# Memory sums from 32-column products, with a new instruction order, in a fused attention and FFN kernel on one Trainium2 core

## The chip, the cores and the metric

The kernel runs on one NeuronCore of a Trainium2 chip. Five engines work side by side and wait for each other through semaphores: TensorE (PE, matrix products into the accumulators of PSUM), VectorE (DVE), ScalarE (ACT), GpSimd (POOL) and SyncE (SP, which only issues DMA transfers here). The metric is device time in microseconds, the median of several executions.

## The reference, cut to what matters

Two pairs of layers follow each other with residual additions: memory attention (A), gated FFN (B), A, B, with the same weights both times. 2048 rows of 512 are worked in four segments of 512 rows; 32 heads of 16 columns.

```python
q, k, v = heads of (layernorm(x) @ wq, wk, wv)
phi = lambda t: jnp.where(t > 0, t + 1.0, jnp.exp(t))
for s in range(N):                    # N = 4 segments
    p = softmax(qs @ ks.T * scale + mask)
    a_dot = p @ vs
    pq = phi(qs)
    num = einsum('bhld,bhde->bhle', pq, M)
    den = einsum('bhld,bhd->bhl', pq, z)[..., None] + 1e-06
    o = g * num / den + (1.0 - g) * a_dot
    pk = phi(ks)
    M = M + einsum('bhld,bhle->bhde', pk, vs)     # the memory sum
    z = z + einsum('bhld->bhd', pk)
x = x + o @ wo
x = x + (gelu(layernorm(x) @ w_gate) * (layernorm(x) @ w_up)) @ w_down
```

M is one 16x16 matrix per head. The change concerns how M is summed, and the order of all the work.

## The kernel before, in words

The whole program is emitted by one function, `order`. It walks through the work with a planner written out by hand: a model clock for each engine (`Clocks`, `Engine`), a list of PE work items (`Item`) with due times and conditions of readiness, and lists of jobs for DVE, ACT, POOL and SP with a slack each. At each step it takes a ready item with the earliest due time and emits its instructions. So the order on every engine, and which engine takes a job that two could do (an eviction from PSUM, a mask, masked copies of k), comes out of the numbers in `POLICY`. On the chip the order is fixed; only semaphores decide the times.

A step `k` (0 to 7) is one segment of one layer pair. Its items on PE are: the q, k and v products; score rounds in row tiling (L938, four products of 16 or 32 rows beside each other); the P·V items, called `flush` (L954), in four column tiles of 32; the memory items `den` (phi(q) by z) and `num` (phi(q) by M); `upd`, the memory sum; `wo`; then `gate`, `up` and `down` of the FFN. `product` (L471 and L476) emits a 128-row product either whole (L476) or as four products in column tiles (L471), after the tiling that PE is in. Where nothing is ready, the planner puts a filling product on a tile of ones, `warm`, into the stream.

The memory sum (`upd_item`, from L853) runs for segments 0 to 2 of each layer. phi(k) is made on ACT and DVE, turned by DMA into `phik` (rows on partitions), and 16 products of 128x128x128 give four blocks of 128x128 in one PSUM bank: each block holds the products of eight heads with eight heads, of which only the eight 16x16 diagonal pieces are wanted. DVE adds the four blocks to `macc` (128x512, float32), and multiplies by the block mask `bd` into `mblk` (L878), which `num` reads; `zcols` (L882) does the same for z, from `zacc`. In segment 0 the mask is applied straight from PSUM, and `macc` is copied afterwards (L893); later segments add to `macc` first (L895).

Layernorm (`Norm`): statistics on DVE (L514, L522), the scale on POOL (L527, L532), `xn` on DVE or POOL (L544), and then a turn into `xnT`, by PE transposes (L586, with evictions at L461 and L462) or by a DMA transpose from SP's queue (L437). `by_pe` decides: the FFN norms of steps 0, 1 and 7, and the input norms up to step `pe_turns`.

SP's queue, in order: the loads of x and of the attention weights, the copies of v into `vz` (L701), the loads of wo, w_gate, w_up and w_down, and the DMA transposes of `phik`, `xnT` and `amT` between them.

## Time and profile before

| | |
|---|---|
| median of 3 runs | 544.17 us (544.15 to 544.77) |
| span of the profiled execution, first to last instruction | 542.6 us (the page gives no other time of that execution) |
| granted TensorE clock | 1.000 of full speed |
| HBM read, written | 9.70 MB, 2.10 MB |
| the costliest group on ACT | exponentials of the scores, 288 of 1026 ns |
| the costliest group on POOL | masks of 256 and 512 columns, 192 together, 579 ns each |
| the costliest groups on PE | 512-column products, 379 ns each by the records, which overlap |

A row of a group reads: line, engine, operation, output <- inputs, partitions x elements, count | busy us, mean ns of one | idle time of the engine just before them, and what ended it. A row of the timeline reads: start and length in us, engine, line, operation, count of merged instructions. Products on PE overlap in the records, so what a run of them takes is read from its start to the start of the next run. Some product records are missing (9271 of 9332).

### The profile page before, as it was taken

The page shows a single profiled execution, that of the slowest core. Times are in us where ns is not written, and L with a number is a line of the kernel's source. Part 1 is how long each engine was busy: PE and PEld are TensorE (multiplying, and loading weights), DVE is VectorE, ACT ScalarE, POOL GpSimd, SP SyncE. Part 2 cuts the span into 40 slices and gives each one's busy share as a digit, 9 for nine tenths or more (in the row PEclk, how much of TensorE's full clock was granted, in tenths as well). Part 3 has the DMA queues.
Part 4 walks back from the last instruction along what each step waited for, and adds up shares of the span by engine and source line. Part 5 has one row for each costly group of instructions (what it writes and reads, how often), then busy time and mean ns, then how long its engine had stood idle before and what let it go on. Part 6 is the DMA issues. An engine that isn't in the chain of part 4 may idle for free.

```text
span 542.6 us, 21272 instructions
## 1 busy us (share of the span) xinstructions
PE 527.1 (97%) x9271; PEld 274.9 (51%) x9332; DVE 443.1 (82%) x816; ACT 434.4 (80%) x540; POOL 305.9 (56%) x359
## 2 busy tenths in 40 slices
PE   8999989999999999999999999999999999999997
PEld 4454455454545444544544555545465456555444
DVE  7898999799988999879987998889586797786342
ACT  6999989988998989989799798996879977930320
POOL 4897786369846788349993468716753265300000
PEclk9999999999999999999999999999999999999999
DMA  8306510610331123310312250211420105100001
GB/s 268 98 13 192 117 23 17 171 35 20 51 50 24 24 40 61 41 38 9 41 32 50 33 71 4 40 33 23 79 52 3 22 13 89 24 3 25 16 0 40
DMA packets 64784, 26.94 MB, mean 50 GB/s; under 512 B 49074, under 2 KB 64690, under 8 KB 64690
## 3 DMA queue, kind: packets, MB, share of 16 engines
q1 hardware_dynamic: 64400, 25.31, 22.7%
q8 instruction: 73, 1.20, 0.9%
q10 hardware_dynamic: 290, 0.26, 0.2%
q14 instruction: 21, 0.17, 0.1%
HBM read 9.70 MB, written 2.10 MB: 22 GB/s over the span
## 4 chain that ended last, share of the span: by engine, by line
PE 83%; DVE 12%; issue 2%; DMA 2%; ACT 0%; POOL 0%; SPq 0%; DVEq 0%; ACTq 0%
PE ps L476 44%; PE ps L471 25%; PE ps L938 7%; PE ps L954 6%; DVE st L514 2%; DVE x_sb L1027 1%; DVE xn L544 1%; DVE byq L971 1%; DMA phik<-e 1%; DVE phiq L745 1%; DVE mv L522 1%; DMA x_sb<-in_A_x_dram 0%; DMA amT<-am 0%; DVE e L745 0%; ACT pt L1398 0%
## 5 line engine op out<-in xcount | busy, mean ns | idle before, releaser
L1398 ACT ACTIVATE pt<-ps 128x1024 bf16<-128x1024 f32 x288 | 279.1, 1026 | 44.3 <-PE ps L938 40.3
L1345 POOL TENSOR_SCALAR_AFFINE_SELECT pt<-pt 128x256 bf16<-128x256 bf16 (+1 forms) x192 | 108.6, 579 | 117.1 <-ACT pt L1398 110.4
L1092 DVE TENSOR_TENSOR gel_sb<-gel_sb,ps 128x512 bf16<-128x512 bf16 x112 | 75.2, 681 | 34.0 <-PE ps L476 25.0
L476 PE MATMUL ps<-xnT,wu_sb 128*128 128x512 bf16 x287 | 66.8, 379 | 1.4 <-issue 1.1
L476 PE MATMUL ps<-xnT,wg_sb 128*128 128x512 bf16 x261 | 62.6, 379 | 1.3 <-issue 0.5
L764 POOL TENSOR_SCALAR e<-e 128x512 bf16<-128x512 bf16 x37 | 57.6, 1557 | 1.6 <-ACT e L741 0.6
L971 DVE STREAM_TRANSPOSE byq<-ps 128x512 f32<-128x512 f32 x64 | 45.0, 706 | 16.3 <-PE ps L954 15.6
L476 PE MATMUL ps<-wd_sb,gel_sb 128*128 128x512 bf16 (+1 forms) x293 | 56.8, 340 | 1.3 <-issue 1.0
L1027 DVE TENSOR_TENSOR x_sb<-x_sb,ps 128x512 bf16<-128x512 bf16 (+1 forms) x68 | 42.8, 640 | 16.5 <-PE ps L476 14.8
L1350 POOL TENSOR_SCALAR_AFFINE_SELECT pt<-pt 64x1024 bf16<-64x1024 bf16 x40 | 47.7, 1194 | 15.1 <-ACT pt L1398 13.8
L471 PE MATMUL ps<-wd_sb,gel_sb 128*32 128x512 bf16 (+1 forms) x792 | 47.1, 378 | 0.6 <-issue 0.6
L476 PEld LDWEIGHTS <-wu_sb 128*128 128x128 bf16 x301 | 28.3, 98 | 33.8 <-issue 0.7
L471 PE MATMUL ps<-xnT,wg_sb 128*32 128x512 bf16 x700 | 42.4, 380 | 0.1
L514 DVE BATCH_NORM_STATS2 st<-x_sb 128x6 f32<-128x512 bf16 x60 | 40.4, 673 | 0.1
L476 PEld LDWEIGHTS <-wg_sb 128*128 128x128 bf16 x273 | 25.3, 98 | 29.1 <-DVE byq L971 0.6
L476 PEld LDWEIGHTS <-gel_sb 128*128 128x128 bf16 x306 | 28.3, 98 | 22.6 <-issue 1.1
L954 PE MATMUL ps<-pt,vaug 128*32 128x256 bf16 (+2 forms) x1344 | 34.8, 238 | 0.3 <-POOL pt L1345 0.3
L471 PE MATMUL ps<-xnT,wu_sb 128*32 128x512 bf16 x588 | 34.1, 379 | 0.0
L417 POOL TENSOR_SCALAR kx<-kf,masks 128x512 bf16<-128x512 bf16 x20 | 33.0, 1649 | 1.2
L1151 ACT ACTIVATE gel_sb<-gel_sb 128x2048 bf16<-128x2048 bf16 (+1 forms) x21 | 33.2, 1643 | 0.0
L954 PEld LDWEIGHTS <-vaug 128*32 128x32 bf16 x1344 | 27.9, 97 | 10.5 <-issue 2.3
L544 DVE TENSOR_SCALAR xn<-x_sb,mv,rs 128x512 bf16<-128x512 bf16 x58 | 31.4, 592 | 2.2 <-POOL rs L532 1.9
(149 smaller groups left out, 877.0 us busy)
## 6 DMA issues: line engine op xcount, KB each, us to landing
vz<-vaug SPq DMA_DIRECT2D x14, 136.0 KB, 2.7
wg_sb<-in_B_w_gate_dram SPq DMA_DIRECT2D x8, 224.0 KB, 4.0
wu_sb<-in_B_w_up_dram SPq DMA_DIRECT2D x8, 224.0 KB, 5.0
wd_sb<-in_B_w_down_dram SPq DMA_DIRECT2D x7, 256.0 KB, 4.7
x_sb<-in_A_x_dram SPq DMA_DIRECT2D x3, 512.0 KB, 6.6
out_dram<-x_sb SPq DMA_DIRECT2D x12, 128.0 KB, 1.9
xnT<-xn SPq DMA_TRANSPOSE x40, 2.5
wk_sb<-in_A_wk_dram SPq DMA_DIRECT2D x2, 256.0 KB, 5.1
```

The lines of the kernel that those rows point to most:

```text
L471: nc.tensor.matmul(out[r], lhsT=lhsT[:, r], rhs=rhs, start=start, stop=stop, tile_position=(0, 32 * c))
L476: nc.tensor.matmul(out, lhsT=lhsT, rhs=rhs, start=start, stop=stop)
L514: nc.vector.bn_stats(out=self.st6[:, 0, :], in_=x_sb[:, self.tt0 + j, :])
L764: lambda eng: eng.tensor_scalar(out=e[0][:], in0=e[0][:], scalar1=1.0, scalar2=None, op0=ALU.min), summed)
L938: nc.tensor.matmul(ps_all[:, bank, o + c0:o + c0 + n], lhsT=lhsT, rhs=self.q[rows, b, q0:q0 + n], start=True, stop=True, tile_position=(32 ...
L954: nc.tensor.matmul(ps()[32 * j:32 * j + 32, q0:q0 + n], lhsT=va[:, ki * VW + g:ki * VW + g + 32], rhs=pt_all[:, places[i], j, c0:c0 + n], ...
L971: nc.vector.transpose(out=self.byq[:, par, :, :].rearrange("p a c -> p (a c)"), in_=ps()[:])
L1027: ck.dve.post(ck.made(), slack, (0.15 + 0.00104 * (c1 - c0), lambda: nc.vector.tensor_tensor(out=xt, in0=xt, in1=ps()[:, 0:c1 - c0], op=AL ...
L1092: ck.dve.post(ck.made(), NORMAL, (0.683, lambda: nc.vector.tensor_tensor(out=g, in0=g, in1=ps()[:], op=ALU.mult), lambda t: (ps.read(t), e ...
L1345: nc.gpsimd.affine_select(out=view, in_=view, pattern=[[0, 4], [0, n], [1, C]], compare_op=ALU.is_ge, fill=0.0, base=C, channel_multiplier=-1)
L1350: nc.gpsimd.affine_select(out=view, in_=view, pattern=[[0, 4 * TPS], [1, C]], compare_op=ALU.is_ge, fill=0.0, base=0, channel_multiplier=-1)
L1398: nc.scalar.activation(out=pt_all[:, s0:s0 + 2, 2 * p:2 * p + 2, :].rearrange("p r h c -> p h r c"), in_=ps_all[:, pair[0]:pair[1] + 1, :] ...
```

## The change

The 16 products of a memory sum become 64: for each block of 128 rows and each group of eight heads, four products of 32 columns, one in each column tile, each multiplying 32 columns of phi(k) (two heads) with the 32 columns of v of the same two heads. The result is 128x128 for all 32 heads (`pairs`), so that `macc` shrinks to 128x128. `spread` then makes the 128x512 `mblk` with the block mask, reading `macc` four times over; segment 0 does so too.

```diff
-    macc = cst.tile([P, 4, P], F32, name="macc")
+    macc = cst.tile([P, 4, 32], F32, name="macc")
...
-            def m(c):
-                j, b = divmod(c, 4)
-                product(blocks()[:, b, :], self.phik[:, j, b * P:(b + 1) * P],
-                        by_head(self.vaug)[:, j, 4 * b:4 * b + 4, :, 0:DH], c == 0, c == n_mm - 1)
+            def m(j, b):
+                ck.tiling("columns")
+                for c in range(4):
+                    nc.tensor.matmul(pairs()[32 * c:32 * c + 32, b, :], lhsT=self.phik[:, j, b * P + 32 * c:b * P + 32 * c + 32],
+                                     rhs=by_head(self.vaug)[:, j, 4 * b + c, :, 0:DH], start=(j == b == 0),
+                                     stop=(j == TPS - 1 and b == 3), tile_position=(0, 32 * c))
+                ck.count += 4
...
-                def gated(src):
-                    return lambda: nc.vector.tensor_tensor(out=made[0][:], in0=src(),
-                                                           in1=bd[:].unsqueeze(1).to_broadcast([P, 4, P]), op=ALU.mult)
+                def spread():
+                    nc.vector.tensor_tensor(out=made[0][:].rearrange("p b (c d) -> p b c d", d=32),
+                                            in0=macc[:].unsqueeze(2).to_broadcast([P, 4, 4, 32]),
+                                            in1=bd[:].rearrange("p (c d) -> p c d", d=32).unsqueeze(1).to_broadcast([P, 4, 4, 32]),
+                                            op=ALU.mult)
...
                 if self.s == 0:
-                    steps = [(0.154, lambda: nc.vector.tensor_copy(out=zacc[:], in_=self.zk[:]), kept),
-                             (0.683, gated(blocks), None),
-                             (Port(0.2), z, told),
-                             (0.683, lambda: nc.vector.tensor_copy(out=macc[:], in_=blocks()), psm.read)]
+                    first = [(0.283, lambda: nc.vector.tensor_copy(out=macc[:], in_=pairs()), psm.read),
+                             (0.154, lambda: nc.vector.tensor_copy(out=zacc[:], in_=self.zk[:]), kept)]
...
+                ck.dve.chain(ck.made(), pol.mem_slack, *first, (Port(0.69), spread, None), (Port(0.2), z, told))
...
-            items.append(Item(lambda: k + pol.upd_due, ready, [(Clocks.MM[128], lambda c=c: m(c)) for c in range(n_mm)],
+            items.append(Item(lambda: k + pol.upd_due, ready,
+                              [(Clocks.SMALL, lambda j=j, b=b: m(j, b)) for j in range(TPS) for b in range(4)],
```

Beside it nearly all numbers of `POLICY` are new, so that the order on each engine is made anew. Some of them are counts: `pe_turns` from 2 to 0 (the input norms of steps 1 and 2 are turned by DMA), `gelu_tiles` from 4 to 7 (tiles of the FFN in one gelu instruction), `hold` from 8 to 3 (score rounds wait until this many gelu tiles are left), `cap` from 4 to 2.

Counted in the instructions of both kernels: products 9332 before, 10075 after; changes of the tiling 301 and 300; column-tiled steps of 512 columns 662 and 808; PE transposes 96 and 64 (16 of each in the first norm); filling products of 128 columns, a column-tiled four counted once, 31 and 44; DMA transposes on SP's queue 88 and 96. In the stretch from the first residual add of the first `wo` to the last `xnT` copy, DVE has the spread, `zcols` and `macc` before, and a second P·V eviction with its reciprocal and scaling after; the spread and `zcols` come behind it.

More of the change, by code (lines that the diff above doesn't have):

```diff
@@ L69 @@
 POLICY = dict(
-    flush_wait=31.348, piece_slack=5.108, kb_slack=25.115, mem_slack=-15.103, margin=2.314, qk_due=0.572,
-    e_q=-1.218, e_k=1.714, exp_slack=-25.107, e_slack=9.023, phi_slack=17.383, gelu_slack=6.274,
-    act_evict=8.464, first_evict=0.965, gate_step=0.061, up_due=-0.553, up_step=0.062, down_due=2.078,
-    down_step=0.526, upd_due=0.786, kb_act=6.552, vz_slack=-10.454, x_dve=-0.565, v0_due=-1.4, x1_at=-45.234,
-    x2_at=18.289, x3_at=24.819, x3_load=-3.83, direct=4, gelu_tiles=4, look=1.769, lag=0.5, wv_at=8.591,
-    xn_pool=7.037, kb_pool=5.303, cut_pool=1.107, at_pool=10.661, pe_turns=2, gate_due=0.765, shun=0.534,
-    col_gap=3.33, hold=8, early=4.123, starve=0.308, near=-1.576, cap=4, soon=9.685, columns=0)
+    flush_wait=60.178, piece_slack=2.474, kb_slack=40.846, mem_slack=-55.59, margin=2.052, qk_due=-2.997, e_q=-1.628,
+    e_k=2.444, exp_slack=-52.211, e_slack=213.844, phi_slack=26.757, gelu_slack=17.711, act_evict=-7.207,
+    first_evict=15.014, gate_step=70.271, up_due=-0.803, up_step=0.121, down_due=2.855, down_step=15.464,
+    upd_due=-0.036, kb_act=30.625, vz_slack=-37.946, x_dve=-2.928, v0_due=-11.201, x1_at=-44.439, x2_at=17.127,
+    x3_at=25.097, x3_load=11.502, direct=4, gelu_tiles=7, look=4.219, lag=0.576, wv_at=-5.253, xn_pool=39.635,
+    kb_pool=0.131, cut_pool=-3.745, at_pool=5.073, pe_turns=0, gate_due=2.262, shun=0.829, col_gap=3.113, hold=3,
+    early=122.612, starve=0.322, near=-0.26, cap=2, soon=21.81, columns=0)
 CHANGES = {
@@ L854, in upd_item, with pairs @@
             psm = Psum()
-            def blocks():
-                return psm().rearrange("p (b d) -> p b d", d=P)
-            n_mm = 4 * TPS
+            def pairs():
+                return psm()[:, 0:4 * 32].rearrange("p (b d) -> p b d", d=32)
             def ready():
@@ L889, in done @@
                 if self.s == 0:
-                    steps = [(0.154, lambda: nc.vector.tensor_copy(out=zacc[:], in_=self.zk[:]), kept),
-                             (0.683, gated(blocks), None),
-                             (Port(0.2), z, told),
-                             (0.683, lambda: nc.vector.tensor_copy(out=macc[:], in_=blocks()), psm.read)]
+                    first = [(0.283, lambda: nc.vector.tensor_copy(out=macc[:], in_=pairs()), psm.read),
+                             (0.154, lambda: nc.vector.tensor_copy(out=zacc[:], in_=self.zk[:]), kept)]
                 else:
-                    steps = [(0.683, lambda: nc.vector.tensor_tensor(out=macc[:], in0=macc[:], in1=blocks(),
+                    first = [(0.283, lambda: nc.vector.tensor_tensor(out=macc[:], in0=macc[:], in1=pairs(),
                                                                      op=ALU.add), psm.read),
                              (0.154, lambda: nc.vector.tensor_tensor(out=zacc[:], in0=zacc[:], in1=self.zk[:],
-                                                                     op=ALU.add), kept),
-                             (Port(0.69), gated(lambda: macc[:]), None),
-                             (Port(0.2), z, told)]
-                ck.dve.chain(ck.made(), pol.mem_slack, *steps)
-            items.append(Item(lambda: k + pol.upd_due, ready, [(Clocks.MM[128], lambda c=c: m(c)) for c in range(n_mm)],
+                                                                     op=ALU.add), kept)]
+                ck.dve.chain(ck.made(), pol.mem_slack, *first, (Port(0.69), spread, None), (Port(0.2), z, told))
+            items.append(Item(lambda: k + pol.upd_due, ready,
+                              [(Clocks.SMALL, lambda j=j, b=b: m(j, b)) for j in range(TPS) for b in range(4)],
                               done, kind="upd", ps=psm, after=("phik", k, 3)))
```

## The prediction

> **What bounds the kernel now.** I read the head of the page first, then the chain of waits, then the windows.

> ```profile
> span 542.6 us, 21272 instructions
> PE 527.1 (97%) x9271; PEld 274.9 (51%) x9332; DVE 443.1 (82%) x816; ACT 434.4 (80%) x540; POOL 305.9 (56%) x359
> ...
> PE 83%; DVE 12%; issue 2%; DMA 2%; ACT 0%; POOL 0%; SPq 0%; DVEq 0%; ACTq 0%
> ```

> TensorE (PE) is busy 97% of the span and carries 83% of the chain that ended last. So a change is worth what it takes out of PE's own row of work, or out of the waits of PE that are left. The windows show where those are.

> ```profile
> 60.00:84.00 24.00, 21.71 (x505) 12.82 (x509) 23.33 (x47) 21.40 (x28) 19.32 (x21) 1.00 0.19 31
> ...
> 130.00:140.00 10.00, 8.51 (x211) 5.13 (x212) 9.77 (x21) 8.36 (x11) 7.50 (x11) 1.00 0.01 3
> 140.00:300.00 160.00, 157.52 (x2894) 80.06 (x2915) 139.46 (x250) 146.74 (x178) 107.80 (x116) 1.00 0.24 39
> 300.00:460.00 160.00, 157.53 (x3082) 83.21 (x3095) 131.00 (x230) 135.13 (x162) 88.94 (x110) 1.00 0.23 39
> ```

> Columns after the stage: PE, weight loads, DVE, ACT, POOL. Between 140 and 460 us PE idles 5 us in 320, a floor of 1.5% spread evenly. Two stretches idle far more: 2.3 us of 24 before the first FFN and 1.5 us of 10 before the second. In both DVE is busy 97 to 98%: there PE waits for layernorm on DVE. Everywhere else the sum is PE's own instructions.

> **Part 1: the products of the memory sums.** Six sums (segments 0 to 2 of both layers) are made. Now each is 16 products of 128 columns; afterwards each is 64 products of 32 columns, four column tiles at a time. The cost of a run is read from its start to the start of the next row in the timeline.

> ```profile
> 264.42 1.14 PE L476 MATMUL ps<-vaug,phik 128*128 128x128 bf16 x16
> 265.40 1.46 PE L476 MATMUL ps<-wd_sb,gel_sb 128*128 128x512 bf16 x5
> ...
> 395.11 1.19 PE L471 MATMUL ps<-vaug,phik 128*32 128x128 bf16 x64
> 396.07 0.65 PE L471 MATMUL ps<-wd_sb,gel_sb 128*32 128x512 bf16 x7
> ...
> 288.41 0.69 PE L471 MATMUL ps<-zcols,phiq 128*32 128x8 bf16 x64
> 288.93 1.27 PE L471 MATMUL ps<-xnT,wu_sb 128*32 128x512 bf16 x20
> ...
> 145.04 0.56 PE L476 MATMUL ps<-zcols,phiq 128*128 128x8 bf16 x16
> 145.46 2.10 PE L476 MATMUL ps<-xnT,wg_sb 128*128 128x512 bf16 x8
> ```

> A sum costs 0.98 us whole and 0.96 us in column tiles now. No product 32 columns wide in four column tiles is in the trace. Nearest below is the 8-wide one: 64 in 0.52 us, 8.1 ns each. Nearest above is the 128-wide one, 0.96 us, which would be no gain. I take 0.52 us, since 32 columns are much nearer to 8 and the narrow run is plainly held by issue and not by its columns: 6 x (0.96 - 0.52) = **-2.6 us**, bounds -2.6 and 0; a loss would need column tiles that don't overlap (rival b).

> [...]

> **Part 2: what the sum becomes on DVE.** The accumulation shrinks from 512 to 128 columns, the masked spread always starts from SBUF.

> ```profile
> L878 DVE TENSOR_TENSOR mblk<-macc,bd 128x512 bf16<-128x512 f32 x4 | 3.9, 970 | 0.0
> ...
> L789 DVE SCALAR_TENSOR_TENSOR rdm<-ps,tmp_e 128x128 f32<-128x128 f32 x6 | 1.7, 281 | 0.0
> ...
> L878 DVE TENSOR_TENSOR mblk<-ps,bd 128x512 bf16<-128x512 f32 x2 | 1.3, 667 | 0.0
> L893 DVE COPY macc<-ps 128x512 f32<-128x512 f32 x2 | 1.3, 666 | 0.0
> ```

> A 128-column read of PSUM takes 0.28 us (row L789) in place of 0.67, six times: -2.3 us of DVE; two spreads go from 0.67 to 0.97: +0.6. The spread stands one instruction later in segment 0, so its readers (the phi of the next segment) see it some 0.3 us later. All of this lies beside dense products: 0 on PE, except in the stretch before the first FFN (part 5). With that cover gone, the 1.7 us that DVE saves would come off the end too, and the later spread would put 0.3 us back per layer.

> **Part 3: products that change form or vanish.** The new order has 300 changes between whole, row and column tiling where the old has 301: 0. It makes 146 more of the 512-column steps in column tiles; the chain of waits prices both forms.

> ```profile
> 473.44 22.45 PE ps L471 x416
> ...
> 515.74 10.96 PE ps L476 x50
> ```

> 416 / 4 = 104 column steps in 22.45 us are 0.216 us each; 50 whole ones in 10.96 us are 0.219, with some records missing: 0.

> The input norms of segments 1 and 2 are no longer turned on PE but by DMA (80 transposes of this line become 48).

> ```profile
> 20.52 1.06 PE L586 MATMUL ps<-ident,xn 128*128 128x128 bf16 x16
> 21.41 0.28 PE L476 MATMUL ps<-warm 128*128 128x128 bf16 x2
> ```

> 16 took 0.89 us; 32 fewer: **-1.8 us**, and eight evictions less on ACT and DVE, beside PE's work: 0.

> The filling products (on a tile of ones, issued where the plan has nothing else) grow from 31 to 44 (column ones counted in fours).

> ```profile
> L476 PE MATMUL ps<-warm 128*128 128x128 bf16 x19 | 2.6, 220 | 0.0
> ```

> A 128-column product costs 0.06 us as above: 13 x 0.06 = **+0.8 us**; the waits that they stand in are counted below. At most, 2.6 / 19 = 0.14 each, +1.8.

> **Part 4: the start of segment 1, now behind eight DMA transposes on SP's queue.** SP's new order is one transpose, the two vz copies, six transposes, then the wo load.

> ```profile
> 17.72 1.40 DVE L544 TENSOR_SCALAR xn<-x_sb,mv,rs 128x512 bf16<-128x512 bf16 x3
> ...
> 18.84 1.35 SPq L701 DMA_DIRECT2D vz<-gel_sb  x2
> ...
> L437 SPq DMA_TRANSPOSE xnT<-xn x40: 1189/1220/2255, 38.3 to 449.3; - x40
> ...
> DMA to landing us min/median/max: 2.4/2.5/4.9
> ```

> DVE's order is unchanged up to these xn. The first is there at about 18.3; SP spends 1.22 us on it (19.5), 1.35 on vz (20.9), then three more; the fourth is issued at 23.3 and lands 2.5 us later, 25.8 (at worst 28.2). The first q product, which needs all four, stands behind 12 v steps (2.6 us), two P·V items, four score blocks and 12 fillings, counted from 20.52.

> ```profile
> 144.04 0.63 PE L954 MATMUL ps<-pt,vaug 128*32 128x256 bf16 x24
> ...
> 144.71 0.40 PE L938 MATMUL ps<-q,kx 32*128 32x256 bf16 x12
> ```

> P·V takes 0.67 us, a score block 0.33 (to 145.04): 20.52 + 2.6 + 1.3 + 1.3 + 0.7 = 26.4, after the 25.8. So the cover just suffices: **+0.4 us**, bounds 0 and +1.8 (28.2 - 26.4). wo and the FFN weights behind them are needed 35 us later: 0.

> **Part 5: the two stretches bound by DVE, and the rest of the order.**

> ```profile
> 74.18 0.65 DVE L878 TENSOR_TENSOR mblk<-ps,bd 128x512 bf16<-128x512 f32 x1
> ...
> 75.35 0.64 DVE L882 TENSOR_TENSOR zcols<-bd,zacc 128x32 bf16<-128x32 f32 x1
> ...
> 76.43 0.67 DVE L893 COPY macc<-ps 128x512 f32<-128x512 f32 x1
> ...
> 78.46 1.06 DVE L461 COPY xnT<-ps 128x512 bf16<-128x512 bf16 x3
> ...
> 79.45 0.70 DVE L971 STREAM_TRANSPOSE byq<-ps 128x512 f32<-128x512 f32 x1
> ...
> 80.58 0.69 DVE L979 TENSOR_TENSOR ab<-byq,r 128x512 bf16<-128x512 f32 x1
> ...
> 80.13 1.89 PE L476 MATMUL ps<-xnT,wg_sb 128*128 128x512 bf16 x7
> ...
> 131.29 0.65 DVE L1027 TENSOR_TENSOR x_sb<-x_sb,ps 128x512 bf16<-128x512 bf16 x1
> ```

> The row at 80.13 is the first gate product, which ends this stretch. Before it, spread, zcols and macc (2.0 us) and one xnT copy (0.35) leave the stretch or move behind it; a byq with its reciprocal and scaling (79.45 to 81.27, 1.8) and the small macc copy (0.28) enter: -0.3. Counted with the prices above, PE has 0.3 us more of other work there as cover: -0.6 in all. Before the second FFN one residual add leaves (0.65), one xnT copy enters (0.35), -0.3, but 0.7 us of PE's cover goes elsewhere: +0.4. Together **-0.2 us**, bounds -1.6 (PE's waits halved, of the 3.8 us idle there) and +1.5 (both gains fail and the lost cover counts twice). Before the first down projection seven fillings stand where one filling and the sum of segment 1 (0.96 us) covered: **+0.4 us**, bounds 0 and +1.3 (the cover lost, 0.96, and six more fillings). In the rest (seven gelu tiles to an instruction, other turns for masks, evictions, gates) counts on DVE, ACT and POOL hardly change, and PE waits little today; for new small waits I take **+0.6 us**, bounds -0.8 (a sixth of the 5 us of idle goes) and +4 (it nearly doubles).

> **Sum:** -2.6 - 1.8 + 0.8 + 0.4 - 0.2 + 0.4 + 0.6 = -2.4: span 540.2. The median of the runs stands 1.6 us above the profiled span (544.17 against 542.6; the page has no other time for that execution), so **541.8 us**.

> **Rivals.** *(a) Attention's pace holds, slower.* After the last score block the new order leaves 329 dense steps where the old leaves 317, 12 x 0.216 = 2.6 us more. So attention must end earlier.

> ```profile
> L1398 ACT ACTIVATE pt<-ps 128x1024 bf16<-128x1024 f32 x288 | 279.1, 1026 | 44.3 <-PE ps L938 40.3
> ...
> 468.14 0.40 PE L938 MATMUL ps<-q,kx 32*128 32x256 bf16 x12
> ```

> If its last block cannot come before 468.1, set by ACT's exponentials and POOL's masks with PE waiting for slots, the end moves by +2.6: 546.8. For it: POOL's and ACT's load above is high until 460. Against: ACT waited 40.3 us for scores, so it has slack. It decides once ACT's waits for scores fall near nothing. *(b) Column tiles don't overlap at this width:* 64 x 26 ns (the whole 8-wide products) = 1.7 us a sum, +4.3 instead of -2.6: 548.7; against it stands the 8.1 ns. [...] *(c) The gain is eaten:* PE arrives earlier and waits for the same DVE and DMA, so the transposes' 1.8 us and a part of the small waits come back, about 544. *(d) Better:* waits before both FFNs shrink to the lower bound and no small wait comes: 541.8 - 1.4 - 0.6 - 0.4 = 539.4.

> **How the numbers follow.** Forecast 0.54 (own range 540.0 to 543.1), (d) 0.13, (c) 0.13, (a) 0.15, (b) 0.05. About 0.2%, 1.1 us, can be told from no change: faster is below 543.1, slower above 545.3. Faster 0.54 + 0.13 = 0.67; same 0.13; slower 0.20. The range 538.9 to 545.4 takes in (c) and (d) and leaves out (a) and (b).

> **What would show it.** Part 1: a run of 64 such products in about 0.5 us; 1 us or more proves it wrong. Part 2: macc rows at 0.28 us. Part 4: the first q of segment 1 near 26.4 us, no PE wait on xnT by DMA. Part 5: the first gate products about 2 us earlier than today's 80.1 (the transposes are gone by then, and half a microsecond of the sum), idle of PE in both stretches no more than now. Rest: the floor of 1.5% idle between 140 and 460 us; a growing idle with ACT or POOL as releaser, and a last score block not before 465, would be (a). Wrong altogether if PE's instructions take as long as now.

## The result and the profile after

| | before | after |
|---|---|---|
| median of 20 runs each, side by side | 544.33 us (543.77 to 545.06) | 543.12 us (542.21 to 544.91) |
| span of the profiled execution | 542.6 us | 541.6 us |

The ratio is 0.9979, with a 95% interval of 0.9972 to 0.9987: the kernel became 1.2 us faster, half of the forecast 2.4 us. A second set of runs of the same kernel (e1 below) gave 0.9972. Executions with a mean granted clock below 0.998 are longer here, by 0.1 to 2.2 us between the medians of a kernel; where they are more than half (e6 to e9, e11), the text goes by the traces.

The head of the page after, and its chain of waits by engine:

```profile
span 541.6 us, 22747 instructions
...
PE 522.7 (97%) x10016; PEld 274.0 (51%) x10075; DVE 439.1 (81%) x814; ACT 434.3 (80%) x533; POOL 297.4 (55%) x346
...
PE 88%; DVE 6%; issue 2%; ACT 1%; DMA 1%; POOL 0%; ACTq 0%; DVEq 0%; POOLq 0%
```

PE's own work shrank by 4.4 us (527.1 to 522.7), more than the forecast 3.6 (2.6 of sums and 1.8 of transposes, less 0.8 of fillings); 0.5 of it are the warm-up products at the very start, 12 in 4.82 us after and 5.30 before, which the change doesn't touch, and a few records are missing in both. But the span shrank by 1.0 only. So PE waits some 3.4 us longer. The windows say where (columns as in the prediction):

```profile
0.00:20.00 20.00, 17.37 (x136) 8.21 (x139) 15.06 (x42) 14.26 (x25) 12.29 (x24) 1.00 0.61 187
20.00:60.00 40.00, 37.86 (x783) 19.47 (x787) 37.88 (x78) 38.51 (x53) 29.94 (x33) 1.00 0.69 145
60.00:84.00 24.00, 22.61 (x570) 13.38 (x571) 22.19 (x44) 22.40 (x30) 19.27 (x22) 1.00 0.25 62
84.00:130.00 46.00, 45.03 (x874) 23.23 (x876) 42.03 (x75) 43.42 (x51) 34.89 (x35) 1.00 0.30 66
130.00:140.00 10.00, 8.51 (x253) 5.58 (x249) 9.74 (x20) 8.32 (x12) 7.13 (x11) 1.00 0.01 3
140.00:300.00 160.00, 157.42 (x3187) 80.81 (x3194) 138.99 (x258) 143.82 (x174) 97.10 (x105) 1.00 0.24 42
300.00:460.00 160.00, 155.82 (x3337) 82.64 (x3351) 129.77 (x230) 139.52 (x164) 90.82 (x112) 1.00 0.23 39
```

The same windows of the kernel before, for the stages that the prediction doesn't show:

```profile
0.00:20.00 20.00, 18.23 (x137) 8.54 (x140) 15.36 (x44) 14.58 (x25) 12.28 (x24) 1.00 0.59 184
20.00:60.00 40.00, 39.22 (x665) 20.05 (x671) 37.29 (x77) 39.28 (x55) 33.89 (x37) 1.00 0.47 131
```

Length less PE's busy time is its idle time. From 20 to 60 us it grew from 0.8 to 2.1 us, from 300 to 460 us from 2.5 to 4.2; before the first FFN it fell from 2.3 to 1.4; in the other stages from 84 to 300 us it kept within 0.2 (from 84 to 130 us it was 0.8 before, with 45.21 busy). The 0.9 us more ahead of 20 us are no loss of the change: the warm-up products ended sooner and the first input landed 0.4 us later in this execution, and PE's first score block stands 0.3 us later, at 10.55 us instead of 10.22. So there are two losses, each in its own place.

The first, in the timeline of PE after (in brackets the idle time ahead of a row, and what ended it):

```profile
21.98 0.30 PE L471 MATMUL ps<-warm 128*32 128x128 bf16 x8 [0.19 <-ACT wd_sb L462]
...
24.31 0.22 PE L476 MATMUL ps<-warm 128*128 128x128 bf16 x1 [0.16 <-ACT pt L1399]
...
25.73 0.41 PE L939 MATMUL ps<-wd_sb 16*128 16x64 bf16 x24 [0.28 <-ACT pt L1399]
26.95 1.05 PE L471 MATMUL ps<-wv_sb,xnT 128*32 128x512 bf16 x16 [0.82 <-DMA xnT<-xn]
```

PE waits four times, 1.45 us in all, 0.82 of it for a norm of segment 1 that DMA turns; the other three are for ACT, its evictions and exponentials. None of the four is in before. The third of the DMA transposes, which ends the longest wait, was issued at 22.68 us and took 4.2 us to land (timeline of SP and view of the DMA, cut to 22.6 to 23.9 us):

```profile
22.68 1.22 SPq L437 DMA_TRANSPOSE xnT<-xn  x1
...
xnT<-xn SPq DMA_TRANSPOSE x1, 4.2
```

The second loss, in the same view, around a memory sum and its neighbours:

```profile
374.22 0.67 PE L866 MATMUL ps<-vaug,phik 128*32 128x32 bf16 x64
374.71 0.64 PE L955 MATMUL ps<-pt,vaug 128*32 128x256 bf16 x24
375.16 0.31 PE L955 MATMUL ps<-pt,vz 128*32 128x64 bf16 x16
375.27 0.41 PE L471 MATMUL ps<-mblk,phiq 128*32 128x128 bf16 x16
375.50 1.05 PE L471 MATMUL ps<-wd_sb,gel_sb 128*32 128x512 bf16 x16
376.48 0.40 PE L939 MATMUL ps<-q,kf 16*128 16x64 bf16 x12
376.81 0.61 PE L955 MATMUL ps<-pt,vaug 128*32 128x256 bf16 x21
378.48 0.26 PE L955 MATMUL ps<-pt,vaug 128*32 128x192 bf16 x3 [1.05 <-issue]
...
406.61 0.29 PE L939 MATMUL ps<-q,kf 16*128 16x64 bf16 x6 [0.41 <-issue]
```

The first two rows give the price of a new sum: 374.22 to 374.71, 0.49 us for 64 products. Then PE stops for 1.05 us in the middle of an item, after 21 of its 24 products, with all inputs there: no semaphore ended the pause, so it is put down to "issue", and semaphores alone don't decide the times here. At 406 us the same happens for 0.41 us. Before had one such stop, where the row ahead begins at 396.07:

```profile
397.34 1.04 PE L471 MATMUL ps<-wd_sb,gel_sb 128*32 128x512 bf16 x13 [0.62 <-issue]
```

The view of the DMA queues of after, cut to 375.5 to 378.0 us (40 slices of 0.06 us; busy share in tenths), has a single packet, of a queue whose kind the view gives as "instruction":

```profile
DMA  0000000009000000000000000000000000000000
...
DMA packets 1, 0.02 MB, mean 7 GB/s; under 512 B 0, under 2 KB 0, under 8 KB 0
...
q8 instruction: 1, 0.02, 2.3%
```

It starts at 376.1 us and takes 2.3% of 16 engines over 2.5 us, 0.92 us. The page after counts 79 such packets (1.29 MB, 16 KB each) for 10075 weight loads and as many products of PE, 20150 instructions, 255.1 to a packet; before has 73 for 18664, 255.7. 256 to a packet, the last one not full, gives both counts; that these packets carry PE's instructions is read from these counts. That made the theory that the experiments test.

### The profile page after: what moved, and what is told of

Its sections match the earlier page's. It is cut to its first block, busy times and chain, and to the rows that moved or that the text cites. A ratio compares the mean times of both kernels' runs of the same rounds, so it can differ in the third digit from the quotient of the medians.

```text
span 541.6 us, 22747 instructions
## 1 busy us (share of the span) xinstructions
PE 522.7 (97%) x10016; PEld 274.0 (51%) x10075; DVE 439.1 (81%) x814; ACT 434.3 (80%) x533; POOL 297.4 (55%) x346
## 3 DMA queue, kind: packets, MB, share of 16 engines
q8 instruction: 79, 1.29, 1.0%
## 4 chain that ended last, share of the span: by engine, by line
PE 88%; DVE 6%; issue 2%; ACT 1%; DMA 1%; POOL 0%; ACTq 0%; DVEq 0%; POOLq 0%
PE ps L476 39%; PE ps L471 34%; PE ps L939 8%; PE ps L955 7%; ACT pt L1399 1%; DVE xn L544 1%; DMA xnT<-xn 1%; DVE st L514 1%; DVE x_sb L1028 1%; DMA x_sb<-in_A_x_dram 1%; PE ps L866 1%; DVE kx L417 0%; DVE st L1184 0%; DVE pt L1356 0%; DVE byq L972 0%
## 5 line engine op out<-in xcount | busy, mean ns | idle before, releaser
L476 PE MATMUL ps<-wd_sb,gel_sb 128*128 128x512 bf16 (+1 forms) x287 | 58.7, 351 | 1.5 <-issue 1.3
L471 PE MATMUL ps<-xnT,wg_sb 128*32 128x512 bf16 x916 | 56.1, 380 | 0.1
L476 PE MATMUL ps<-xnT,wu_sb 128*128 128x512 bf16 x213 | 51.1, 379 | 1.5 <-issue 1.1
L476 PE MATMUL ps<-xnT,wg_sb 128*128 128x512 bf16 x207 | 49.9, 379 | 1.6 <-issue 1.4
L471 PE MATMUL ps<-xnT,wu_sb 128*32 128x512 bf16 x888 | 51.0, 379 | 0.0
L471 PE MATMUL ps<-wd_sb,gel_sb 128*32 128x512 bf16 (+1 forms) x816 | 45.3, 361 | 0.0
L476 PEld LDWEIGHTS <-gel_sb 128*128 128x128 bf16 x300 | 27.9, 98 | 25.3 <-issue 0.4
L1351 POOL TENSOR_SCALAR_AFFINE_SELECT pt<-pt 64x1024 bf16<-64x1024 bf16 x26 | 32.4, 1247 | 9.8 <-ACT pt L1399 9.0
L471 PEld LDWEIGHTS <-wu_sb 128*32 128x32 bf16 x888 | 23.0, 97 | 22.3 <-issue 0.9
L476 PEld LDWEIGHTS <-wu_sb 128*128 128x128 bf16 x226 | 20.8, 98 | 24.8 <-issue 1.2
L471 PEld LDWEIGHTS <-wg_sb 128*32 128x32 bf16 x916 | 23.4, 97 | 19.1 <-issue 1.3
L1152 ACT ACTIVATE gel_sb<-gel_sb 128x3584 bf16<-128x3584 bf16 (+1 forms) x14 | 32.4, 2351 | 0.0
L939 PE MATMUL ps<-q,kx 32*128 32x64 bf16 (+2 forms) x1120 | 31.2, 217 | 0.7 <-ACT pt L1399 0.5
```

The source lines that it names most:

```text
L471: nc.tensor.matmul(out[r], lhsT=lhsT[:, r], rhs=rhs, start=start, stop=stop, tile_position=(0, 32 * c))
L476: nc.tensor.matmul(out, lhsT=lhsT, rhs=rhs, start=start, stop=stop)
L939: nc.tensor.matmul(ps_all[:, bank, o + c0:o + c0 + n], lhsT=lhsT, rhs=self.q[rows, b, q0:q0 + n], start=True, stop=True, tile_position=(32 ...
L1152: return (0.205 + 0.427 * (f1 - f0), lambda: nc.scalar.activation(out=g, in_=g, func=ACT.Gelu_apprx_tanh), lambda t: self.gelu_done(t, f0, ...
```

## The experiments

Four theories. **S**: the narrow sums are worth what the forecast said, about 0.44 us each. **O**: the new order, without them, is where the gain or the loss is. **C**: PE stops because it has run out of fetched instructions. **N**: the stops are chance, or belong to the instructions they stand before. Each kernel keeps the order of all instructions that its edit doesn't touch, on every engine, so that one thing changes at a time; each is compared with runs of the kernel before on the same chip.

**e1: the kernel after, once more.** No edit.

> The changed kernel once more, beside the next three on one chip. Its first profile shows PE standing for 1.05 us at 377.4 us in the middle of a P·V item, with no semaphore to wait for (ended by issue). Theory C (PE runs out of fetched instructions after a dense stretch): the gap is at the same place again, about 1 us. Theory N (a chance disturbance): it is elsewhere or not there. Both: about 1.2 us below the kernel before. The start of segment 1 (third v item of that segment, 26.95 us) waits for its DMA transpose again by both.

Measured: 542.64 us (before 544.38), ratio 0.9972 [0.9963, 0.9982]. The timeline of PE:

```profile
26.41 1.05 PE L471 MATMUL ps<-wv_sb,xnT 128*32 128x512 bf16 x16 [0.55 <-DMA xnT<-xn]
...
377.37 0.27 PE L955 MATMUL ps<-pt,vaug 128*32 128x192 bf16 x3 [0.79 <-issue]
```

Both losses are there again at the same instructions, smaller by 0.27 and 0.26 us. So they belong to the kernel; of chance is only their size.

**e2 and e3: after's order with the old sums.** e2 makes them of 16 whole products, e3 of 64 products of 128 columns in column tiles; both take the wide `macc` with them. The line shown is e3's.

```diff
-                                     rhs=by_head(self.vaug)[:, j, 4 * b + c, :, 0:DH], start=(j == b == 0),
+                                     rhs=by_head(self.vaug)[:, j, 4 * b:4 * b + 4, :, 0:DH], start=(j == b == 0),
```

> The new order on every engine, but each memory sum by 16 whole products of 128 columns, macc 512 columns wide, as in the kernel before. Theory S (the sums are worth what the prediction said, 0.44 us each, and each whole sum between column-tiled neighbours adds changes of tiling, 9 in all by count, about 0.1 us each): 6 x 0.46 + 0.9 = 3.7 us over the changed kernel, that is 2.5 us over the kernel before. Theory C: the same, but with 576 fewer PE instructions the gap at 377 us closes and gives about 1.1 us back: 2.6 us over the changed kernel, 1.4 us over the kernel before.

> The new order, each memory sum by 64 products of 128 columns in column tiles, macc 512 wide. As many PE instructions as the changed kernel, no other changes of tiling. Theory S: 6 x 0.44 = 2.6 us over the changed kernel, 1.4 us over the kernel before. Theory C: the sum's instructions are spread over 0.96 instead of 0.52 us, so the gap at 377 us shrinks by up to 0.4 us: 2.2 us over the changed kernel. If the sums had cost as much as before in their new form (rival b of the prediction), no difference.

Measured: e2 545.67, ratio 1.0025 [1.0014, 1.0036]; e3 545.38, ratio 1.0016 [1.0008, 1.0025]. In one order the narrow sums are worth 545.67 - 542.64 = 3.0 and 545.38 - 542.64 = 2.7 us, 0.46 to 0.5 each: S holds. (The differences hold the unlike stops of the kernels too; by the traces alone an unbroken sum takes 0.49 us in after and 0.97 to 1.02 in e3.) And the new order alone is **slower** than the old, by 1.0 to 1.3 us. (The 0.1 us for a change of tiling stands in PE's timeline of before: eight whole products ahead of one take 1.83 us, from 13.59 to 15.42; four with none behind them 0.87, from 18.79 to 19.66.) The stops, from the timeline of e2:

```profile
406.09 0.38 PE L471 MATMUL ps<-zcols,phiq 128*32 128x8 bf16 x33 [0.69 <-issue]
...
410.19 0.22 PE L476 MATMUL ps<-mblk,phiq 128*128 128x128 bf16 x1 [0.54 <-issue]
```

With fewer instructions in the sums the stops stand before other work than in after. e3, which has as many instructions as after, still stops at the later of after's two places (at 408.74 us, for 0.67 us) and at a new one at 344.59, but not at the earlier place, where its sum takes twice as long.

**e4: before's order with the new sums.** Only the products of the sums and the DVE steps behind them are after's.

```diff
+                for c in range(4):
+                    nc.tensor.matmul(blocks()[32 * c:32 * c + 32, b, :], lhsT=self.phik[:, j, b * P + 32 * c:b * P + 32 * c + 32],
+                                     rhs=by_head(self.vaug)[:, j, 4 * b + c, :, 0:DH], start=(i == 0),
+                                     stop=(i == n_mm - 1), tile_position=(0, 32 * c))
```

> The kernel before with its order on every engine kept, only the products of the memory sums and their DVE steps in the new form. Theory S: -2.6 us on PE, and 6 more changes of tiling (four sums stand between whole products) at 0.1 us: 2.0 us below the kernel before. Theory C: the same, but 200 to 400 more PE instructions can open a new gap of about 1 us: 1.0 us below. Theory O (the gain of the change comes from the new order and not from the sums): no difference from the kernel before.

Measured: **541.70 us** (541.52 to 541.77), ratio 0.9950 [0.9938, 0.9962]. It beats both kernels; beside them on one chip it is 2.7 us under before and 0.9 under e1. Its windows where after lost:

```profile
20.00:60.00 40.00, 39.21 (x664) 20.00 (x671) 37.30 (x76) 39.28 (x55) 33.80 (x37) 1.00 0.48 131
...
300.00:460.00 160.00, 158.16 (x3162) 83.18 (x3175) 131.00 (x233) 136.44 (x163) 91.53 (x113) 1.00 0.21 39
```

Idle 0.8 and 1.8 us, against 2.1 and 4.2 in after. It has no stop in its timeline that lasts over 0.2 us; the one of before at 396 us is gone too. So part of its 2.7 us is that stop (0.6), which the edit did not aim at; the other 2.1 are what S named, 2.0.

**e5: the vz copies off SP's queue.** After, with the two copies of segment 0 that stand ahead of the DMA transposes started by POOL.

```diff
-                        ck.sp.post(ck.pe, pol.vz_slack, (0.62, lambda a=a: nc.sync.dma_start(
+                        ck.sp.post(ck.pe, pol.vz_slack, (0.62, lambda a=a: (nc.gpsimd if k == 0 else nc.sync).dma_start(
```

> The kernel after, with the two vz copies of segment 0 started from POOL's queue instead of SP's; nothing else. In the kernel after PE stands still for 0.82 us at 26.1 us until the DMA-turned norm of segment 1 has landed, and the transposes stand behind the two vz copies (1.35 us of SP) in SP's queue. Theory Q (the queue sets the start of segment 1): the transposes are issued 1.3 us earlier, the wait on xnT at 26 us is gone or under 0.2 us, and the time is 0.5 to 0.8 us under the kernel after, about 542.4. Theory L (the norms on DVE or the landing of a transpose set it, not the queue): the wait stays within 0.2 us of 0.3 to 0.8 and the time with it, 543.1.

Measured: 543.49 us, ratio 0.9985 [0.9974, 0.9995]. The wait is gone, and the time is no better. Seven transposes now run from 18.20 us in one row of SP, and the v products start at once (timelines of SP and of PE):

```profile
18.20 13.51 SPq L437 DMA_TRANSPOSE xnT<-xn  x7
...
25.73 0.41 PE L939 MATMUL ps<-wd_sb 16*128 16x64 bf16 x24 [0.28 <-ACT pt L1399]
25.79 1.05 PE L471 MATMUL ps<-wv_sb,xnT 128*32 128x512 bf16 x16
```

So Q was right on the wait and wrong on the time. Set beside e1 instruction by instruction, e5 is 0.63 us ahead at these v products; then it falls back in four steps, by 0.24 at 31 us, 0.16 up to 172, 0.24 at 341 and 0.22 at 405, and is 0.23 behind from there on. The last two are places where instruction packets end, ahead of PE's instructions 13236 and 16050 (180 and 178 modulo 256; the count stands below e12). The first is a P·V item that waits 0.15 us for ACT's exponentials in e5 and not in e1. The cause of the second isn't shown.

**e6: no fillings.** The 44 filling products left out of after (their result isn't read).

```diff
-                product(ps()[:, 0:P], warm[:], wide[:, 0, :])
```

> The kernel after without its 128-column filling products (44, column ones counted in fours). Only products of the ones tile are left out, whose result nobody reads. Term of the forecast: 13 more fillings cost 0.8 us, 0.06 us each, so all 44 are 2.6 us of PE's time. If the fillings cost what they take: 543.1 - 2.6 = 540.5. Theory W (each stands in a wait that is there anyway): PE's busy time falls by 2 to 3 us and its idle time grows by as much, the time stays within 0.5 us of 543.1. If the granted clock falls in the longer pauses, it gets slower than 543.6.

Measured: 541.88 us (541.64 to 542.64), ratio 0.9959 [0.9946, 0.9971]. Faster than the first set of after; from e1's ratio it isn't told apart, as the intervals overlap. Neither named time came out, 540.5 nor 543.1 within 0.5. The gain is not by the fillings: at the start of segment 1 what they took is waited instead, and the v product that waits for the norm starts at 26.95 us as in after.

```profile
26.95 1.05 PE L471 MATMUL ps<-wv_sb,xnT 128*32 128x512 bf16 x16 [1.00 <-DMA xnT<-xn]
```

The first gate product comes at 79.06 us instead of 78.80, and a score block that after has at 134.52 comes at 135.26; but between 75.1 and 78.5 us the granted clock of this execution was 0.50 (0.93 in the window from 60 to 84), so that these two rows can't be put down to the fillings alone. All of the gain over after falls behind 140 us. In e6 220 PE instructions fewer move where the packets end; no stop is left at 377 us in its timeline, and that at 406 us is smaller:

```profile
405.36 0.27 PE L955 MATMUL ps<-pt,vz 128*32 128x64 bf16 x12 [0.23 <-issue]
```

Whether the fillings keep the granted clock up stays open: without them its mean was below 0.998 in 14 of 17 executions (e6, e11), with them in 7 of 43 (after, e1, e5), but in 7 of 12 of e9 too.

**e7: the stretch before the first FFN, relieved on DVE.** Before, with `zcols` of the first sum on POOL and its `macc` copy on ACT.

```diff
-                    nc.vector.tensor_tensor(out=made[1][:], in0=bd[:, 0:P:16].unsqueeze(1).to_broadcast([P, 4, 8]),
+                    (nc.gpsimd if k == 0 else nc.vector).tensor_tensor(out=made[1][:], in0=bd[:, 0:P:16].unsqueeze(1).to_broadcast([P, 4, 8]),
```

> The kernel before, with two DVE instructions of the first sum that stand in the stretch before the first FFN given away: zcols (0.64 us) to POOL, the first copy of macc (0.67 us) to ACT. Theory D (DVE sets the end of this stretch, as the forecast of the new order assumed): the first gate product comes 0.9 to 1.3 us earlier than 80.13, the time is about 543.2. Theory A (attention's exponentials and masks, or the norm's chain, set it): the first gate product stays within 0.3 us of 80.1, the time within 0.4 us of 544.3; POOL's zcols may even come late for the first state product, then up to 1 us slower.

Measured: 544.96 us, ratio 1.0016 [1.0007, 1.0024]: slower. The timelines of PE and of DVE (the first row is the kernel before, at the same item):

```profile
77.16 0.27 PE L938 MATMUL ps<-q,kf 16*128 16x64 bf16 x5 [0.45 <-DVE macc L893]
...
77.57 0.27 PE L939 MATMUL ps<-q,kf 16*128 16x64 bf16 x5 [0.87 <-ACT macc L893]
...
80.55 0.81 PE L476 MATMUL ps<-xnT,wg_sb 128*128 128x512 bf16 x2
...
78.33 1.10 DVE L461 COPY xnT<-ps 128x512 bf16<-128x512 bf16 x3 [0.75 <-PE ps L586]
```

Both edits were one kernel; but DVE, relieved of 1.3 us, now stands 0.75 us idle and waits for PE, while PE waits 0.87 us for ACT's copy of `macc`, where it waited 0.45 us for DVE's. From this item to the first gate product it is 2.97 us before (77.16 to 80.13) and 2.98 in e7 (77.57 to 80.55): the 0.4 us by which that product is later are the later copy. So it isn't DVE's load as a sum that ends this stretch, but PE's own row from the item that waits for this copy; what the stretch would gain with an earlier copy, this run doesn't show. Theory D is out; of A the mechanism stands, but its bounds, 0.3 us for this product and 0.4 for the time, are passed by 0.1 and 0.3.

**e8: the norms turned by DMA without the new order.** Before, with the norms of segments 1 and 2 given to DMA at the place where PE turned them; 32 transposes of PE and 8 evictions left out.

```diff
+                if not by_dma:
+                    nc.tensor.transpose(turned()[:, kt, :], xn()[:, kt * P:(kt + 1) * P], ident[:])
+                elif kt == 0:
+                    nc.sync.dma_start_transpose(out=self.xnT[:, :, j * P:(j + 1) * P], in_=xn()[:])
```

> The kernel before, in its own order on every engine, with the input norms of segments 1 and 2 turned by DMA at the place where PE turned them: 32 transposes (0.056 us each, 1.8 us) and eight evictions of 0.35 to 0.6 us are left out, eight DMA transposes of 1.2 us stand on SP. Term of the forecast: -1.8 us on PE and, at the start, up to +0.4 to +1.8 of waiting. Here the q, k and v products stand as close behind the turning as they did for PE, nothing is moved ahead as cover. Theory T (a DMA transpose is late, 2.5 us to landing behind 1.2 us each on the queue): PE waits 2 to 5 us on xnT by DMA between 20 and 60 us, the time is 545 to 548. Theory G (the cover that is there already suffices): PE waits less than 0.5 us on it, the time is 542.5.

Measured: 548.72 us, ratio 1.0083 [1.0068, 1.0098]; theory T, and a little worse. The timeline of PE:

```profile
23.15 1.46 PE L476 MATMUL ps<-wv_sb,xnT 128*128 128x512 bf16 x3 [1.66 <-DMA xnT<-xn]
...
36.05 1.02 PE L476 MATMUL ps<-xnT,wq_sb 128*128 128x512 bf16 x3 [1.17 <-ACT pt L1404]
...
42.17 1.04 PE L476 MATMUL ps<-xnT,wq_sb 128*128 128x512 bf16 x3 [1.16 <-DMA xnT<-xn]
```

What PE saves, 1.8 us, comes back more than twice as waits. The granted clock fell to 0.96 of full speed between 20 and 60 us besides. The new order puts other work into most of these waits, not into all.

**e9, e10, e12: the same program, its instructions counted differently.** Two of the twelve warm-up products at the very start, which run before the first input is there, become 42, 98 or (in e4's kernel) 66 products of 8 columns. All later instructions stay what and where they are, with a number that is 80, 192 or 128 higher.

```diff
-    keep_warm(WARM, 0)
+    keep_warm(WARM - 2, 0)
+    for i in range(42):
+        c = slice(32 * (i % 4), 32 * (i % 4) + 32)
+        nc.tensor.matmul(ps_all[c, 0, 0:8], lhsT=warm[:, c], rhs=warm[:, 0:8], start=True, stop=True,
+                         tile_position=(0, 32 * (i % 4)))
```

> The kernel after with 80 more PE instructions (rows: weight loads and products) at its very start: of the 12 warm-up products of the ones tile two become 42 products of 8 columns, all before the first input is there. Nothing else changes; every later instruction only has a row number that is 80 higher. PE's instructions come in packets of 256 rows. In the kernels after, e1 and e5 PE stood without a releaser before rows 14772 (0.8 to 1.05 us, at 377 us) and 16050 (0.2 to 0.4 us, at 405 us), both 178 to 180 rows past a multiple of 256. Theory C (PE has run out of fetched rows there): the boundaries move 80 rows up in the program; the 256 rows that end at the new one near 372 us ran in 1.7 us in e1 (stops fell on blocks of 2.1 to 2.7 us), so there is a stop of 1 us or more at 372 us, none at row 14772 + 80, and the one at 405 us is gone or smaller. Time 543 to 544. Theory N (the stops belong to those instructions or their data): they stay before the same products, 377 and 405 us, time 542.6 to 543.1.

> As e9, with 192 more rows at the start (98 narrow products for two warm-up products). Theory C: the boundaries move 192 rows up; by the times of e1 the quickest block after 140 us is then the one that ends near 399 us (2.6 us), all others take 3.1 us or more; so there is no stop at 372 to 377 us and none at 405 us, at most one of up to 0.8 us at 399 us. Time 0.3 to 1.2 us under the kernel after, 541.9 to 542.8. Theory N: stops before the same products as in the kernel after, time 542.6 to 543.1.

> The kernel of e4 (before's order with the new sums, 541.70, no stop over 0.2 us without a releaser) with 128 more rows at its start, made as in e9. Theory C: by the times of e4 the 256 rows that end at the new boundaries near 169 us and 392 us ran in 1.7 and 1.5 us, under all blocks that stopped PE so far; so PE stops at both places, 0.7 us or more each, and the time is 543.0 to 544.5. Theory N: as e4, 541.5 to 541.9.

Measured: e9 543.69 us, 0.9990 [0.9974, 1.0007]; e10 543.03, 0.9974 [0.9965, 0.9984]; e12 544.21, 0.9996 [0.9988, 1.0005]. The timelines of PE, e9 first, then e10:

```profile
376.59 0.61 PE L475 MATMUL ps<-wd_sb,gel_sb 128*32 128x512 bf16 x7 [0.24 <-issue]
```

```profile
403.02 0.39 PE L475 MATMUL ps<-zcols,phiq 128*32 128x8 bf16 x31
404.26 0.38 PE L475 MATMUL ps<-zcols,phiq 128*32 128x8 bf16 x33 [0.85 <-issue]
```

And e12, whose parent e4 has no such stop:

```profile
172.53 0.28 PE L877 MATMUL ps<-vaug,phik 128*32 128x32 bf16 x14 [0.53 <-issue]
...
397.12 2.56 PE L475 MATMUL ps<-wd_sb,gel_sb 128*32 128x512 bf16 x44 [1.00 <-issue]
```

The stops moved with the count, in e12 to the two blocks that C named. The instructions that after stopped at run through in e9 and e10. N falls. The sizes were called less well: e9's stop is 0.62 us from start to start where 1 or more was expected, and at 376.59 us, where 372 was named for this packet end (e9 runs from 542.07 to 547.33 us, too spread for its time to tell C from N); e10 has one of 1.03 where at most 0.8 was, and is no faster than e1, where 541.9 to 542.8 was expected (in its profiled execution the granted clock was 0.50 from 136.5 to 139.8 us, 0.83 in the window from 130 to 140, and PE took 8.61 us from the score block at 133.49 to the product at 142.10, 1.4 more than the 7.21 in after). Not all of e12's 2.5 us over e4 is stops: PE's first k products ran slower (4 in 1.06 us; 0.60 in e4), the q products behind them too (8 in 1.40 us; 1.04 in e4), and PE reached 33 us 1.1 us late. e9 and e10, which lack the same two wide warm-up products, lost nothing there, so that this loss isn't shown to come from the edit. The two stops make up the rest (1.5).

Here are the pauses of 0.6 us or more between two successive product starts behind 140 us, found by laying each trace beside the list of PE's instructions; where the packet landed is from the packets of the trace:

```
kernel   restart us   paused   instructions before it   modulo 256   packet landed   to restart
before     397.34      1.00          14260                180           395.90         1.44
after      378.48      1.29          14772                180           377.03         1.45
after      406.61      0.61          16050                178           405.22         1.39
e1         377.37      1.04          14772                180           375.90         1.47
e2         406.09      0.86          15284                180           404.70         1.39
e2         410.19      0.76          15538                178           408.72         1.47
e3         344.59      0.78          13236                180           343.18         1.42
e3         408.74      0.87          16050                178           407.52         1.22
e5         377.38      1.04          14772                180           375.81         1.57
e7         397.97      0.69          14260                180           396.72         1.25
e9         376.59      0.62          14772                180           375.10         1.49
e10        404.26      1.03          16052                180           402.96         1.30
e11        377.46      0.97          14516                180           375.89         1.58
e12        172.53      0.71           6076                188           171.15         1.38
e12        397.12      1.38          14772                180           395.74         1.37
```

Fourteen of fifteen stand at the same place of a packet of 256 (the fifteenth is among 64 like products with records missing, where the count is not exact), and in all of them PE starts again 1.2 to 1.6 us after a packet landed. From 140 to 462 us the fourteen traces have 702 such packet ends, and the median stretch of 256 instructions between two takes 6.2 us. Of the 28 stretches under 2.75 us, 13 were followed by one of these pauses; of the other 674, two were. So in these traces the stops stand where both come together, a packet's end and a quick stretch ahead of it. It is what theory C expects; that PE has run out of fetched instructions there is an inference, as how many it has left can't be seen in the traces.

**e11: e5 and e6 together.** Both edits in the kernel after.

> The kernel after with the edits of e5 (the two vz copies of segment 0 started from POOL's queue) and e6 (no 128-column filling products). e6 alone gave 541.88, and PE still waited 1.0 us for a DMA-turned norm at 26 us; e5 took this wait away. If what stands at the start is carried to the end: 541.0 to 541.4, under the 541.70 of before's order with the new sums. If it comes back later, as it seems to in e5 (no faster than the kernel after): 541.9.

Measured: 543.09 us (541.55 to 547.65), ratio 0.9988 [0.9969, 1.0007]; too spread to say more than that it doesn't beat e4. At the packet end near 377 us, which e6 passed with 0.38 us between two products, there is a stop of 0.69 us by the timeline:

```profile
377.46 0.53 PE L955 MATMUL ps<-pt,vaug 128*32 128x256 bf16 x20 [0.69 <-issue]
```

## Why the prediction was half right

**Part 1, the sums: right.** 0.49 us for each unbroken sum in after (three of the six; in e4, where a sum stands between whole products, 0.60), as against 0.52; 2.7 to 3.0 us in all by e2 and e3, forecast 2.6. 64 in 0.49 us are 7.7 ns each, where the 8-wide ones of before take 8.1 in column tiles and 26 whole (16 from 145.04 to 145.46 us): 32 columns cost no more than 8. That such a run is held by issue was the author's inference; the rows show only these times. Rival (b) is out.

**Part 2, DVE: right.** The last accumulation of the sum above, in DVE's timeline of after, takes the forecast 0.28 us to a hundredth, and all six `macc` rows take 0.27 to 0.29; the spread, taken as 0.97, has a median of 1.06 us, and the view names no wait for it:

```profile
375.42 0.27 DVE L897 TENSOR_TENSOR macc<-macc,ps 128x128 f32<-128x128 f32 x1
```

**Part 3: the work fell as forecast, the sum did not.** The transposes left PE, but e8 shows that their 1.8 us can't be entered apart from the waits of Part 4. The 0.8 us for more fillings was counted wrongly as far as the start of segment 1 shows: they stand in waits there, and without them (e6) PE arrives no earlier, at 26.95 us.

**Part 4, the start of segment 1: the first step that failed.** It said +0.4, with the wait at the first q product, behind the fourth row. Measured are 1.2 (e1) to 1.45 us. The wait came one item earlier, at the last v products ahead of q, which need the third block of rows; and the P·V and score items that were to be its cover themselves waited for ACT, 0.6 us. "No PE wait on xnT by DMA" was wrong in after, e1, e2 and e3. The bounds, 0 to 1.8, held it. The term reckoned 2.5 us from issue to landing, the median of its row; the third transpose took 4.2. Issued at 22.68 us, it would have landed at 25.2 by the 2.5, ahead of the 26.13 us at which PE stood ready (an estimate from these rows). e5 shows that an earlier place in the queue takes this wait away too, and that this alone wins nothing at the end; why the landing took so long isn't shown.

**Part 5: better and worse.** Before the first FFN idle fell by 0.9 us (forecast 0.6), the first gate product came 1.3 us earlier rather than 2, as the start had lost 1; its reason, DVE's load, is not borne out by e7, where PE's row behind the copy of `macc` decides. Before the second FFN nothing changed (forecast +0.4); in the stage of the first down projection it is +0.2 (forecast +0.4). **"The rest of the order", +0.6, is the second step that failed**: between 300 and 460 us alone it is 1.7 us, of which 1.05 and 0.41 are the stops without a releaser at a packet's end, less the 0.62 that before had. Most of the rest are short pauses ahead of whole products. The view of PE's waits in this stage (us in total, times, longest), before and then after:

```profile
PE ps L476 <- issue: 1.3, 8, 0.2
```

```profile
PE ps L476 <- issue: 2.2, 14, 0.2
```

All of these pauses stand where PE goes from score blocks back to whole products: 8 of 26 such changes before, 14 of 26 after. Why more of them cost something stays open. The forecast looked for small waits on DVE, ACT and POOL, and took the pauses put down to "issue" for a fixed cost; its "floor of 1.5% spread evenly" already held one stop of 0.62 us in one place, at 397 us. Rival (a) is out too: the last score block stands at 464.57 us, before 465 by a little, and between 140 and 460 us the view of PE's waits in after has none on ACT or POOL.

Added up by runs: the order was to cost 0.2 us (all terms but the sums) and costs 1.0 (e3 against before) or 0.9 (e1 against e4). That and the better sums give e1's -1.7 us. The first set of runs of after lies another 0.5 us higher, inside the spread that start and stops have from one execution to the next (the two profiled ones lie 1.3 us apart: 0.3 by the first input, 0.3 by the wait on xnT, 0.7 at three packet ends). Rival (c), "the gain is eaten, about 544", is nearest to what happened, but of the engines that it named only DMA took part, with the one wait of 0.55 to 0.82 us.

Open is also what sets the size of a stop (of the 28 quick stretches 15 passed with less than 0.6 us, in e8 one of 2.2 us with 0.2), and e5's step back up to 172 us.

## What to carry to other kernels

The narrow products bought PE time here (0.49 us a sum, 0.97 to 1.02 in e3) and made the stretches of instructions around them quicker: count how long each stretch of 256 PE instructions lasts. Every stop of the table followed one that ran in 1.5 to 3.3 us, and 80, 192 or 128 instructions more at the start (e9, e10, e12) moved the stops to other stretches, so judge a small gain in more than one alignment. Try a local improvement in the old order as well before you take a new order with it: here the old order with the new sums is the best kernel measured, 541.70 us. A part of that is luck: e12 is the same order and the same sums with 128 instructions more at the start, and takes 544.21.
